# Agent attention and a SoLU feed-forward layer on one core: another table for the order of all queues

## The chip, the core and the metric

The kernel runs on one NeuronCore of a Trainium2 chip. The metric is device time in microseconds (us); lower is better. The core has five queues that work side by side and meet only at semaphores: TensorE (PE in the profile; its weight loads are PEld), VectorE (DVE), ScalarE (ACT), GpSimd (POOL) and SyncE (SP), which starts the transfers. Each queue takes its instructions strictly in the order in which the program wrote them: an instruction that waits holds up all that stand behind it on its queue.

## The reference

The inputs are q, k, v of 4 batches x 12,608 tokens x 128 channels and 49 agents for each batch.

```python
def _attn_ref(q, k, v, agents):
    scale = 1.0 / np.sqrt(q.shape[-1])
    def sm(a, b):
        s = scale * (a @ b.transpose(0, 2, 1)); s = s - s.max(-1, keepdims=True)
        e = np.exp(s)
        return e / (e.sum(-1, keepdims=True) + 1e-09)
    return sm(q, agents) @ (sm(agents, k) @ v)

def _moe_ref(x, w_in, w_out, g_ln):          # x: 50,432 tokens x 128
    h = x @ w_in                              # 128 -> 1024
    e = np.exp(h - h.max(-1, keepdims=True))
    solu = h * (e / (e.sum(-1, keepdims=True) + 1e-09))
    mu = solu.mean(-1, keepdims=True); var = ((solu - mu) ** 2).mean(-1, keepdims=True)
    return ((solu - mu) / np.sqrt(var + 1e-06) * g_ln) @ w_out   # 1024 -> 128
```

## The kernel before

**Tiles.** The 50,432 tokens are 394 tiles of 128 tokens, x = 0 to 393. For each tile the kernel goes through the same steps, each on its own queue:

- hidden layer (TensorE, L956, in two halves): `ph` = 128 x 1024, one PSUM buffer for even tiles and one for odd ones
- max (VectorE, L984): reads `ph`, writes `e_a` or `e_b` (even, odd tile) and the tile's extreme value
- exp (ScalarE, L991): reads `e`, writes the exponentials back into `ph` and sums them
- product (VectorE, L999): `u` = e x `ph`, into one of six buffers `u_a` to `u_f`, and its sum. With it `ph` and `e` of this tile come free, and the hidden layer of tile x+2 may start
- square (ScalarE, L1020): the sum of squares for the variance; it may come several tiles later
- turning `u` over: for 331 tiles it is split into two float16 parts (GpSimd or ScalarE L1007/L1005, then GpSimd L1010, buffers `f_a` to `f_e`) and turned by a transposing DMA (SP, L1014) into `x_a` to `x_h`; for the other 63 tiles TensorE turns it in two halves (L1027) and ScalarE or VectorE copies it out of PSUM (L1032) into `t_a` to `t_h`
- second layer (TensorE, L1048): 24 float16 matmuls from `x`, or 8 float32 ones from `t`, into a PSUM bank `px` that four tiles share; written in pieces, between which other work may stand
- for every 8 or 16 tiles a chain of tiny steps for 1/sqrt(var) (ScalarE and GpSimd, L1063 to L1086), and for every four tiles the scaling into `ob` (VectorE, L1093) and a store (L1099)

**Beside it.** For the next batch, in 13 chunks, the agents' attention over k and v (L585 to L755: loads, TensorE L602, L635, L655, VectorE L607 to L664, ScalarE L619, L628, L645); and for every 8 tiles the softmax of q over the agents (L843 to L911: `logits`, `pack`, its transposed form `pT`, copied out by ScalarE or VectorE). Batch 0's agents' attention and the conversion of the weights (L399 to L509) have nothing to stand beside: they are the head of the program, about its first 56 us.

**What sets the order.** `op(...)` declares 7,003 steps: a queue (or a choice of two, `eng` with two letters), a function that writes the instructions, and the steps it depends on. `Plan.run` then goes through a table, `STEPS`, a packed list of pairs (step, which of its two queues), and writes the steps in that order:

```python
        for i, k in todo:
            o = self.ops[i]
            e = o.eng[k]
```

Nothing else sorts them: priorities, costs and due times that stand in the code (`DH`, `DMX`, `due`, ...) do not decide the order, since the table does. The planned times in `run` choose two things only: which of four free PSUM banks a step takes, and how many filler matmuls (`idle`, L1109) stand before TensorE's steps in the head. The lines that the change and the prediction touch are L956, L984, L991, L999, L1020, L1048 and the table.

Of the kernel before, what the change touches and what calls it, by code (L numbers as in the profile page):

```python
# [18 lines left out]
AF = mybir.ActivationFunctionType  # L19
# [11 lines left out]
    "MzeXE>Azps4`{~4QL^=PaL@m6uqKtN&VK06m20N#(ck`0zG>y?Q6{RX>A=Ax*1w`5G&}0m2;NpZ1b{Dc7a6o<woHk5R3rNKY$YN4?tiG<)<hS#"
    "#77HLa{cA`SiEs+bZtTsY-=D|(h)<bk?bWSp=#go!jxmSMr8<yHP;$ybY@{IiH|jdWcSpdE4?^yGa^g&kB`Lq=K+3Wh@EK^1a+E=P_}ogBOgxP"
    "CoAvQ0!Kh2Yp+$#`;Hb<hEqbn=Ue=}KkaFXHArRiZ$FHj%E@7T0}TG`PoIa}nLhQ7MU7LZs>&%_xWlrKrSaW^Mo;%_x4mtM0PC|h*;=c7x3ZJG"
    "v&^;XcCF5I+5@EhE9+?mbpj^szx_M-E!A?~+;lKu)^yfu!&eQ52eJt;P~DzBTBKrUiI%yK<n+5H{YnFHbP%#xA0W&++5QwTu3(4Kd0U&QSFz-t"
    "@m;&##S~-*0EX2ny^|c!hMlfHOsAP#OgpV<a^g1KN|95!@Xfm8igXTWt*J4~6{*_NU$+0@*VjhJj>#iANvziCWa)cyBBlb<R|5%BF=gH|VS&X-"
    "@XP;m<gV(J(pX)x6|XkDuU{VO93lGxeM5b5u<3Cmk4Adi7H$;nvC00i^OW&Yc?~LLYhCMJJ(=w%<)`v-_n|Q@tBz?e$xZ-p*;eP~ATZ%UeP3Em"
    "4Uu2_snD8i4Hx$`Uo`D^S4qO!$3Ga|ArpiP*yrwpX#*J8vDeL9)q2hEdQ_?4v3J(tXf|e3aLuFDHjf>QS1rv>F3vhGSDaurN7mct>~n_xxR^?L"
    "=Cp(}7))8s{&;-!hE(kI+Z{69_N1qOxjv+>@LjJMjSUZV9r0kl&wfFiHf-lCmyOtE<2}{jpSXM=wNsXUvp-hTvPQN>bSWjZa=jM4e~?T3wrFti"
    "Sbs_G-N{EU8`m0+f8?juCcq&HTEIluNLUC^?Wh`WINa{sBCDGEgDOP>7{AA;m8BzWArUf3o4~g1^c;Fu%|}wDT9idBRxhw64`Mi&S1u-%H>c_2"
    "zDR9r#btPG#v@&&`VVD|%g)TUqD^*FGo&5M`RwgSk+_4j`i|Oxl&tlPfyInF>$O!Zn^!-?(_yMUdQUjg3oSYj?4O@poC};m+xX8r^!LP$cFE$n"  # L40
    "omrYc^7!U$R*iL7ZfG2O2p-6q3=PZeReRft6B)jGq4I3Y^c!QHedb)xrDx0^Q(ek_^!uHM@<vxnQifL&W37Yt%E?gr?yh~kz5aH(J!oogG}X?g"
    "Yp(HAthvgf75&_G_2P8p?Hw`c^%yH-s%bw+e$aMaNb2$9ww?M++PioXn={*2Tn7rU5-0p{rO=`GkNb{~+s(i8U+g!k?d7ZORo9RIT1)z5@a}ZW"
    "PMQ-fcjV!R#f!)o4scc7)XkA*UU&X+=HjHT1DFrCx2inOY3u6J#JaXxX?9-ik1m-e7cbSROIhX0TgU9XQ+cPX@%_}ol&!<^AOGvb1rAOIE*ov>"
    "fXxv-p2~DwHH07Z;NZjo4m&}gRi2PZyZoCWWnJj}L(jyFyk#q$86pQ-C(TnsotqUK0aMy8?eyCxdk#0+MrH3O8$+{e<XdU~$#vJBcv`mI7y-=^"
    "jgnG#%^t_<=8ZwQ8@Ei3?O9d12Ib(w)Pgc>(9g=}f(K*|?zP_LPRSvBrcLijcLP~Y;gQcRB;@k5&I2-&?&&`0^58>w+wlf|Gq@yw^J6m#JZX!Q"
    "#A(fNRI^7W-0y2^$>AlRF%w$A4b{t`57VvDMW1Qbf7P%sWn3BDRrpo5c`$k{ac&!dTW0aw`XY;e_}!RntmS=hI~6+Yyy)<of$cJQoY5XS|H)4n"
    "T*QYxeVx4OzCPv*gTC>8?Gl6%ur#qBHn>CkgNL#DP7kGdr*8kw*G{ZX<=8>v!7MOArjeh{_Kh|l_U=kYkJq)*;|TzUfOW1fGi%!J-CZBHsj1zK"
    "?s%nptVX@z>FrJeDdw_lMfa(R@$A-c3*NJnlE}uLitha#;;i$ucX!cT)qJB!0&q4HP<L&?5r90SNVcri^^&JV1_w*ak=9#q_GiC#tVp+jHQiO~"
    "jb?1AT|7R&sE&Jwap0I$#4E47{lWPrJgn*6^SSWqkM5uUAA?s7lS><WAZhAY0`s={%`4K8ovfdpYaItmI?8|Klr;dm7dU_Pt4#HJPE`|_zEupb"
    "oydIss`yr?4q7KI)`Fdn0~a0J13Ij&!MxUpCtHq2&fQ~)!K78;Y4#`v_qzc>5jh_@F+=)5jYpbP{KIb~BDE)EdSvuNB=Bw;-+UNdm@}k}^WlX$"  # L50
    "=?bBV2KEAdJyo&jQSklk>>hdIGIyEw$)USOP1Lxu5pHV%Ew#puo+LiI*wt?w^eDQGE3GLPE*k`ZsBPCs=lk6nquY~^?%<kUM^={_nbxJooi0m-"
    "zPHA=H@+|x0?t^#7BEEhxhwrapw?ya4U7)$;b!stro<NMO$=Q0Cz~Tg)#PksZ(+&}$;Yq?f1G5$E@bh^Omo_W%z#I}>eJbX@#xveLidtJQuQx>"
    "&1sTF4i|PbnGUaY>tr<7g8THRV%d3P;@F#(fpyu5_!^%wwGm^GAi(`$Le{^(c4YSJdfyH;Dt3AriI#V=9a}JcRHxo*I_h%|7~|^1#HRE%KHE<i"
    "WYcrjuGuqE4*=LB$4vokc%1|aO1(JKuOnns_e78EWJ?wACuE&ot7a^1b@V}#pGGD-w+F!4ul$lcJ>**5JnMA7zx7(ddecWekluzrrqz*&vmblf"
    "Xpq4Tc(?uMe`jN8uV?Q4+w1x|Ad4qj=j<1QL7f7$*tN3eyMSrVs2ZMc=!@9q2PePteQ#TB=#Vf?`L{O*?YjQ{pwZ-CIn((EW@V|kO;@v)lzO`q"
    "vPSv5v1yS~WICWk!T0-`-E+q$WH(_p>^k?m*P*i>DJm?!52O`eJ#2&SoCr8`+RK}4?a6T%94AxLd-^S}?kZw@sFwHao}|)sJ@1q?)nj|aZf_(t"
    "cSh!-wN71V8z%<=ZVGIscdg)1GBs+sksE7j-}=*zr2lQVF?i_HK?5$jw$j$!q+&IGyhn_Dm^e5hGohW#(a-$ru4SjSb-XH~1pU#?u`OlgVcZVY"
    "XzfW|E~2Bn^|~2z!$Zye;+SG*+Y5sy8JMX~He9M=TYX(K^PxSr<Z4+DVJE)fn{mgy|LCW|hmMYc?emqy&;8_Kr^%MMBF#j=H0yPCC?@2TUS;tq"
    "^#;-}9XqP?E`UnU(Sz5uOeNaKmvx(SSN_Y!Wv^;m9<)z*Ku4t21d&YT3T{MGR-!2~?38w<f%YO!2As0A$4IK+(l$P5Jw$6neX&VQ-4S3YcmW#k"
    "!-J-6kcicU%#e9-t9MI=Q}blVX3j-T>z(3n|Kd@f=Q{h&)#H*lx|Vy>J!i5L#pdoZnU1@z*1J{9U^~2}H#oziE0iJ7pl+XkyAt#e@rJ%GWzSFl"  # L60
    "Y25Du`1ZiKMu$`Hvg6yvNsYbpuxCc9@OHJ0o55bso~nZq1JHh!={ozxAH4((=0tbK>2ACQW2yRuj2OR>XW|{#+rjW{WyJ@p7-)&*-}t_js0SZi"
    ";**WKD_KNcd7W0ARl8S5m&vP2^HH+;s_U?)Dg}{88mwvmINtR(?Y7lTxTIu7+&p%DnScP_Bp*~-jt|v0c=BO>J*w1zN%`PqBYx9%*|;9N^<ON%"
    "pIR|1Ck~~nhUQgOMn3D9P@2i6Lmdo`3zww}2lCScDcB*rkuw=J5xOMZ{b@r3xEzbFYe;g$Hny?ptG~#oG)qaK&IA_XO);7Bx=I?5M`nP(yZN9i"
    "TL<x{wXUY)CI<Q{m+C5dX5C9U59R3$JH+5!^LCx<pzEOyc+UnmZkC)Ai>`0~R^(yEJFi_@9-p(1nZTj=x*mAq{)f6al!Z25T)G>dR;BwcA_S0M"
    "ZfhzpqK?1ue`GF=xc;DP!@WrmQALl%xjbvIr+XGPr#V6v@B*K7aR2Orv{oPFx{`QpxK8ho`JjFncFf{KjpE~Me+$@kTT*Xj(cTa4Q~A!&FnPP="
# [1232 lines left out]
```

## Time and profile before

| | |
|---|---|
| median of 3 runs | 1259.42 us (1253.04 to 1260.58) |
| the profiled execution's own time | 1255.41 us, span 1253.6 us |
| granted clock of TensorE, mean over the span | 0.997 of full speed |
| busy: PE, DVE, ACT, POOL | 1209.3, 1203.3, 1183.0, 1119.7 us |
| first max of a tile (start of the tiles) | 56.18 us |

A busy time is the time in which at least one instruction of the engine ran. In the timeline a row has its start, its length, and in brackets how long the engine sat idle before it and what ended that. The instruction behind it on DVE or ACT often starts a little before it ends (its last 0.07 us or so overlap), so what an instruction takes on its queue is the distance from its start to the next one's start. The small READ_ACCUMULATOR rows belong to the row ahead of them.

### The profile page before, as it was taken

What the parts mean: (1) busy time and instruction counts of PE and PEld (TensorE: products, weight loads), DVE (VectorE), ACT (ScalarE), POOL (GpSimd) and SP (SyncE); (2) the same over time, 40 slices, a digit from 0 to 9 for tenths busy, and PEclk for the clock granted to TensorE, in tenths of its full rate; (3) what the DMA queues carried; (4) which work ended last, traced back from release to release, by engine and by line L of the source; (5) the groups of instructions that cost most, each with busy time, mean ns of one, the idle gap of its engine ahead of it and who ended that gap; (6) DMA issues with size and microseconds to landing.
All of it is one profiled execution on the core that took longest, in us unless ns stands there. A gap on an engine that the chain in (4) does not pass through costs nothing.

```text
span 1253.6 us, 36378 instructions
## 1 busy us (share of the span) xinstructions
PE 1209.3 (96%) x14304; PEld 933.9 (74%) x14304; DVE 1203.3 (96%) x2296; ACT 1183.0 (94%) x2212; POOL 1119.7 (89%) x889
## 2 busy tenths in 40 slices
...
GB/s 367 201 226 237 216 251 227 218 243 219 203 200 244 250 222 249 249 257 238 226 201 207 247 247 236 231 261 235 214 231 193 174 196 219 166 224 200 194 190 169
DMA packets 721516, 281.41 MB, mean 224 GB/s; under 512 B 692672, under 2 KB 696256, under 8 KB 721344
## 3 DMA queue, kind: packets, MB, share of 16 engines
...
## 4 chain that ended last, share of the span: by engine, by line
PE 24%; DVE 23%; ACT 21%; issue 14%; POOL 10%; DMA 8%; SPq 0%; POOLq 0%; DVEq 0%; ACTq 0%
PE px L1048 10%; ACT ph L991 9%; PE ph L956 7%; DVE e_b L984 4%; DVE e_a L984 4%; ACT sq_a L1020 4%; ACT sq_b L1020 4%; PE px L655 2%; POOL f_b L1010 2%; PE px L602 2%; DVE u_f L999 2%; DVE u_d L999 2%; DVE u_a L999 2%; POOL f_a L1010 1%; DVE u_c L999 1%
## 5 line engine op out<-in xcount | busy, mean ns | idle before, releaser
L984 DVE TENSOR_SCALAR_CACHE_REDUCE e_a<-ph,nk 128x1024 f32<-128x1024 f32 x197 | 251.8, 1278 | 6.5 <-PE ph L956 5.5
L984 DVE TENSOR_SCALAR_CACHE_REDUCE e_b<-ph,nk 128x1024 f32<-128x1024 f32 x197 | 251.9, 1278 | 5.3 <-PE ph L956 4.9
L991 ACT ACTIVATE ph<-e_a,nm 128x1024 f32<-128x1024 f32 x197 | 219.3, 1113 | 16.2 <-DVE e_a L984 14.8
L991 ACT ACTIVATE ph<-e_b,nm 128x1024 f32<-128x1024 f32 x197 | 219.3, 1113 | 9.0 <-DVE e_b L984 8.0
L999 DVE SCALAR_TENSOR_TENSOR u_d<-e_b,cb,ph 128x1024 f32<-128x1024 f32 x66 | 84.3, 1277 | 2.1 <-ACT ph L991 1.6
L999 DVE SCALAR_TENSOR_TENSOR u_a<-e_a,cb,ph 128x1024 f32<-128x1024 f32 x66 | 84.2, 1275 | 1.8 <-ACT ph L991 1.4
L999 DVE SCALAR_TENSOR_TENSOR u_c<-e_a,cb,ph 128x1024 f32<-128x1024 f32 x65 | 82.9, 1275 | 2.4 <-ACT ph L991 1.6
L999 DVE SCALAR_TENSOR_TENSOR u_e<-e_a,cb,ph 128x1024 f32<-128x1024 f32 x65 | 82.9, 1275 | 1.5 <-ACT ph L991 1.1
L999 DVE SCALAR_TENSOR_TENSOR u_f<-e_b,cb,ph 128x1024 f32<-128x1024 f32 x65 | 82.8, 1274 | 1.3 <-ACT ph L991 0.7
L999 DVE SCALAR_TENSOR_TENSOR u_b<-e_b,cb,ph 128x1024 f32<-128x1024 f32 x65 | 83.0, 1277 | 1.0 <-ACT ph L991 0.4
L1048 PE MATMUL px<-wh,x_a 128*128 128x128 f16 x672 | 70.1, 219 | 3.6 <-DMA x_a<-f_e 1.7
L1048 PEld LDWEIGHTS <-x_a 128*128 128x128 f16 x1008 | 61.7, 98 | 14.2 <-DMA x_a<-f_e 1.9
L1048 PE MATMUL px<-wh,x_b 128*128 128x128 f16 x672 | 71.5, 219 | 0.7 <-DMA x_b<-f_a 0.5
L1048 PEld LDWEIGHTS <-x_b 128*128 128x128 f16 x1008 | 61.4, 98 | 14.4 <-issue 5.7
L1048 PE MATMUL px<-wh,x_c 128*128 128x128 f16 x672 | 70.9, 219 | 0.9 <-ACT pT_d L911 0.3
L1048 PEld LDWEIGHTS <-x_d 128*128 128x128 f16 x984 | 60.5, 98 | 14.8 <-issue 2.6
L1048 PE MATMUL px<-wh,x_d 128*128 128x128 f16 x656 | 68.9, 219 | 1.9 <-DMA x_d<-f_c 0.6
L1048 PEld LDWEIGHTS <-x_c 128*128 128x128 f16 x1008 | 61.9, 98 | 11.7 <-issue 2.3
L1048 PEld LDWEIGHTS <-x_e 128*128 128x128 f16 x984 | 60.2, 98 | 13.2 <-issue 3.8
L1048 PE MATMUL px<-wh,x_g 128*128 128x128 f16 x656 | 68.5, 219 | 1.5 <-DMA x_g<-f_e 1.2
L1048 PE MATMUL px<-wh,x_h 128*128 128x128 f16 x656 | 69.2, 219 | 0.6 <-DMA x_h<-f_c 0.6
L1048 PEld LDWEIGHTS <-x_h 128*128 128x128 f16 x984 | 60.5, 98 | 12.4 <-DMA x_h<-f_c 1.1
...
## 6 DMA issues: line engine op xcount, KB each, us to landing
...
```

The lines of the kernel that those rows point to most:

```text
L602: nc.tensor.matmul(px[h * AP2 : (h + 1) * AP2, :w], ag_sb[:, b, :], kt[:, o : o + w], start=True, stop=True)
L655: nc.tensor.matmul(px[h * AP2 : (h + 1) * AP2, :C], eT[:w, o + h * AP2 : o + (h + 1) * AP2], vt[:w, t, :], start=all(z[0] != h for z in mm ...
L956: nc.tensor.matmul(ph[:, sl], w, m[:, sl], start=(q == 0), stop=(q == len(mm) - 1))
L984: nc.vector.tensor_scalar(out=nhs[x], in0=phs[x], scalar1=nks[k][:, j : j + 1], scalar2=None, op0=ALU.mult, op1=ALU.min, accum_out=nms[x])
L991: nc.scalar.activation(out=phs[x], in_=nhs[x], func=AF.Exp, scale=-1.0, bias=nms[x], accum_out=rs_[R]["S"][:, j : j + 1])
L999: nc.vector.scalar_tensor_tensor(out=u, in0=nhs[x], scalar=scal(x)[:, 4:5], in1=phs[x], op0=ALU.mult, op1=ALU.mult, accum_out=su)
L1010: nc.gpsimd.tensor_tensor(out=fs[x][:, 1, :], in0=us[x][0], in1=fs[x][:, 0, :], op=ALU.subtract)
L1020: nc.scalar.activation(out=sq, in_=u, func=AF.Square, bias=su, scale=-float(DF), accum_out=rs_[R]["Q"][:, j : j + 1])
L1048: nc.tensor.matmul(po, ut, wt[:, kf, :], start=(q == 0), stop=(q == len(mm) - 1))
```

## The change

Only the table `STEPS` is another one: 7,003 pairs as before, of the same steps. Two of its lines, one of each side (the rest is alike: packed text):

```diff
 STEPS = (
-    "c-pOb4@@Ipe&6_Eyevy7wWbpvp%fv?@v|)ILxehrB1C;IaU70Vlu$w~$8j8oB0|v?IgU#l*CK>$R|pZ}I+o=Ugf^5CN?gbBITTSssbg`3x;_pe"
...
+    "c-p0T4^V4ge%H+*<nj2iNYm@}{t#J2WNDg7Q<h~JM9Ls$(llidBO)Tj42=w>H1kAcV@xwKrYvP%8N_Ui5hGIO$sj}1l%_GI3}ujFmSQH8vdAzD"
...
 )
```

Unpacked, the two tables agree in their first 3 steps and differ in the order of nearly all queues from there on, the head's included. 85 steps change their queue: 25 of the first splits go from ScalarE to GpSimd and 22 the other way; the copies of `pack` 10 from ScalarE to GpSimd and 9 back; the copies of `pT` 9 from VectorE to ScalarE and 6 back; the copies of `t` 3 from ScalarE to VectorE and 1 back.

**Place 1: TensorE around the hidden layer of tile 46** (201 to 204 us in the trace; `mh`, `ml` are the batch's matrix in two float16 parts, `ph_167` the even tiles' buffer, `x_a`, `x_b` two turned tiles for the second layer). Before:

```order
L956 LDWEIGHTS pT_b
L956 MATMUL ph_167<-mh_655,pT_b 128x512
L956 LDWEIGHTS pT_b
L956 MATMUL ph_167<-ml_656,pT_b 128x512
L1048 LDWEIGHTS x_a
L1048 MATMUL px_170<-wh_93,x_a 128x128
...
L1048 LDWEIGHTS x_b
L1048 MATMUL px_170<-wh_93,x_b 128x128
L956 LDWEIGHTS pT_b
L956 MATMUL ph_167<-mh_655,pT_b 128x512
```

and now:

```order
L1048 LDWEIGHTS x_b
L1048 MATMUL px_172<-wh_93,x_b 128x128
L956 LDWEIGHTS pT_b
L956 MATMUL ph_167<-mh_657,pT_b 128x512
L956 LDWEIGHTS pT_b
L956 MATMUL ph_167<-ml_658,pT_b 128x512
L956 LDWEIGHTS pT_b
L956 MATMUL ph_167<-mh_657,pT_b 128x512
L956 LDWEIGHTS pT_b
L956 MATMUL ph_167<-ml_658,pT_b 128x512
L1048 LDWEIGHTS x_b
```

Before, 12 matmuls of the second layer (six from `x_a`, six from `x_b`) stand between the two halves of this tile's hidden layer; now the halves follow each other.

**Place 2: ScalarE between the exponentials of tiles 227 and 228** (754 to 760 us in the trace; `nm` is the tile's extreme value, `sq` a square's output that nobody reads). Before:

```order
L991 ACTIVATE ph_168,S_10085<-e_b,nm_10512 128x1024
L1032 COPY t_c<-px_172 128x512
L911 COPY pT_b<-px_171 128x512
L1020 ACTIVATE sq_a,Q_10086<-u_e,su_c 128x1024
L1020 ACTIVATE sq_a,Q_10086<-u_c,su_a 128x1024
L991 ACTIVATE ph_167,S_10085<-e_a,nm_10590 128x1024
```

and now:

```order
L991 ACTIVATE ph_168,S_10080<-e_b,nm_10514 128x1024
L1020 ACTIVATE sq_b,Q_10081<-u_b,su_h 128x1024
L1032 COPY t_c<-px_172 128x512
L1020 ACTIVATE sq_a,Q_10081<-u_e,su_c 128x1024
L991 ACTIVATE ph_167,S_10080<-e_a,nm_10583 128x1024
```

The copy of `pT_b` has left this gap; two squares and one copy stand in it still.

**Place 3: ScalarE between the last two exponentials, of tiles 392 and 393** (1236 to 1243 us in the trace). Before:

```order
L991 ACTIVATE ph_167,S_17408<-e_a,nm_17365 128x1024
L1063 ACTIVATE t_17430<-S_17073,cb_13260 128x8
L1032 COPY t_e<-px_169 128x512
L1020 ACTIVATE sq_b,Q_17074<-u_f,su_f 128x1024
L1020 ACTIVATE sq_a,Q_17074<-u_a,su_g 128x1024
L1020 ACTIVATE sq_b,Q_17074<-u_d,su_d 128x1024
L991 ACTIVATE ph_168,S_17408<-e_b,nm_17452 128x1024
```

and now:

```order
L991 ACTIVATE ph_167,S_17405<-e_a,nm_17362 128x1024
L1032 COPY t_e<-px_172 128x512
L1020 ACTIVATE sq_b,Q_17069<-u_d,su_d 128x1024
L1063 ACTIVATE t_17445<-S_17068,cb_13253 128x8
L1020 ACTIVATE sq_a,Q_17069<-u_e,su_e 128x1024
L1020 ACTIVATE sq_b,Q_17069<-u_b,su_h 128x1024
L1020 ACTIVATE sq_b,Q_17069<-u_f,su_f 128x1024
L991 ACTIVATE ph_168,S_17405<-e_b,nm_17457 128x1024
```

Four squares stand in front of the last exponential instead of three, and two behind it instead of three.

## Rows read from the trace of the kernel before

**Rows 1.** The page: span, and busy time of each engine over it.

```profile
span 1253.6 us, 36378 instructions
PE 1209.3 (96%) x14304; PEld 933.9 (74%) x14304; DVE 1203.3 (96%) x2296; ACT 1183.0 (94%) x2212; POOL 1119.7 (89%) x889
```

**Rows 2.** Stretches: length, busy PE, PEld, DVE, ACT, POOL; clock; DMA share, GB/s.

```profile
0.00:60.00 60.00, 49.64 (x467) 30.07 (x468) 43.07 (x115) 32.55 (x77) 23.47 (x33) 0.97 0.76 289
80.00:1240.00 1160.00, 1133.20 (x13567) 882.79 (x13564) 1134.32 (x2137) 1123.45 (x2087) 1075.95 (x834) 1.00 1.06 222
1240.00:1254.00 14.00, 10.36 (x116) 9.94 (x113) 6.53 (x13) 8.11 (x18) 2.23 (x10) 1.00 0.32 123
320.00:420.00 100.00, 98.17 (x1193) 76.25 (x1193) 99.45 (x186) 98.89 (x184) 96.72 (x75) 1.00 1.05 223
420.00:620.00 200.00, 199.53 (x2415) 155.83 (x2412) 196.98 (x374) 194.65 (x371) 184.13 (x145) 1.00 1.14 242
```

**Rows 3.** VectorE's waits: what waited, for whom: us in total, times, longest.

```profile
DVE e_a L984 <- PE ph L956: 5.5, 10, 1.1
DVE e_b L984 <- PE ph L956: 4.9, 10, 1.6
...
DVE pk L718 <- ACT av_dup L714: 2.6, 4, 0.9
DVE row L675 <- PE px L669: 2.4, 1, 2.4
DVE u_c L999 <- ACT ph L991: 1.6, 8, 0.3
...
DVE u_b L999 <- ACT ph L991: 0.4, 2, 0.2
```

**Rows 4.** Timeline at 200 to 204 us: VectorE, then TensorE's hidden layer of tile 46.

```profile
200.70 1.28 DVE L999 SCALAR_TENSOR_TENSOR u_d<-e_b,cb,ph 128x1024 f32<-128x1024 f32 x1
...
203.16 1.28 DVE L984 TENSOR_SCALAR_CACHE_REDUCE e_a<-ph,nk 128x1024 f32<-128x1024 f32 x1 [1.05 <-PE ph L956]
...
201.43 0.38 PE L956 MATMUL ph<-mh,pT_b 128*128 128x512 f16 x1
...
202.53 0.38 PE L956 MATMUL ph<-mh,pT_b 128*128 128x512 f16 x1
```

**Rows 5.** Timeline at 754 to 760 us: ScalarE, then VectorE, tile 228.

```profile
755.07 0.58 ACT L911 COPY pT_b<-px 128x512 f16<-128x512 f16 x1
755.55 1.16 ACT L1020 ACTIVATE sq_a<-u_e,su_c 128x1024 bf16<-128x1024 f32 x1
...
757.97 1.10 ACT L991 ACTIVATE ph<-e_a,nm 128x1024 f32<-128x1024 f32 x1
...
759.11 1.10 ACT L991 ACTIVATE ph<-e_b,nm 128x1024 f32<-128x1024 f32 x1
...
759.23 1.28 DVE L999 SCALAR_TENSOR_TENSOR u_a<-e_a,cb,ph 128x1024 f32<-128x1024 f32 x1 [0.37 <-ACT ph L991]
```

**Rows 6.** Timeline of the end: ScalarE's last exponential, VectorE's last product, TensorE.

```profile
1241.71 1.10 ACT L991 ACTIVATE ph<-e_b,nm 128x1024 f32<-128x1024 f32 x1
...
1242.98 1.28 DVE L999 SCALAR_TENSOR_TENSOR u_d<-e_b,cb,ph 128x1024 f32<-128x1024 f32 x1 [0.60 <-ACT ph L991]
...
1247.67 0.60 PE L1027 MATMUL px<-ident,u_d 128*128 128x128 f32 x4
```

**Rows 7.** Timeline at 885 to 898 us: a transposing DMA, and who waited.

```profile
885.46 4.31 SPq L1014 DMA_TRANSPOSE x_a<-f_e  x1
...
894.26 0.23 PE L1048 MATMUL px<-wh,x_a 128*128 128x128 f16 x1 [1.74 <-DMA x_a<-f_e]
...
897.83 0.48 DVE L675 TENSOR_REDUCE row<-px 1x64 f32<-1x128 f32 x2 [2.38 <-PE px L669]
```

**Rows 8.** Groups by line in the head: busy us, mean ns of one, idle before.

```profile
L399 DVE TENSOR_SCALAR u_e<-u_e 128x512 int32<-128x512 int32 x4 | 4.3, 1080 | 0.0
L399 DVE TENSOR_SCALAR u_a<-u_a 128x512 int32<-128x512 int32 x4 | 1.7, 420 | 0.0
```

More of the change, by code (lines that the diff above doesn't have):

```diff
@@ L31 @@
[L31 to L65, printed above, removed]
@@ new lines @@
+    "ve`Rnj12O4JV@^K+&@X~y|C-3^WKEy-gD1A=lkdL`Fy{p`J}Zgj>V@^9k;r^!!(v|t~g5{_H|&#8{@Y+XG_(lCOVMW?b$t?JgKrC-PLCzt@cIv"
+    "rV7_wWIhZHFNcQ12DE*>(mg4^tGcbfJ;P^xiMII@7r2q>P6k?+=Vz}XGnb}!)%D)C3**k}#!3C*P`j&n$$whuPtUB4RJ9N3<!d9AsN-P<_+}i#"
+    "4Y#Yq+Gy2m`N*2NZE8Gl_V})<Y8Jh*p_u?k-7NV`a=&puet-HQgC>*%ONWM3>R{Irv<+<TrZ;C=2dwFyWZKy@;Uyox@=pQi-<D<j0#d0~o%BnA"
+    "MscP{-FKwoJrNC&%A$2dOq){fXxGV>Yz>N?lZyFK{NMfgBq6^a!q-#y&FJ35o>K0u+chfED`0^fUQ8=@qaazMMMuK#qr)QxZ)&Dnquj%%VyU!J"
+    "r4838=X(~>L^yUHP!g+PZDg8QA0AvXOOF>vQ^PoTJW18mR1-&w3%jAUk>QZvIIy{XH!&YZvxv4F^=Yg9k!H<_F?JHx&ivXpPDATyqB;`L-_P#j"
@@ new lines @@
+    "=#=GVZQW~ir4rVw(J5;JQ%)t8(5a0<0F1ZsC9^Gc(1<GE*9>NwmTw-LYrDHf&nj%Q<~6W(7f?o&J6Fz=U-=%H=-u8iX@EhmRPVa5qX|oN8a=)-"
+    "%%+o};g*_#Sq*u1(sJXq&YlwKuKgweh>#ELgU*e1wWH4()bAWy#!>Q-tc>q0JQ7Fvp*4jyjqDtToLlm<iGxo4G?qwpuh+K|hM)egU;RxY?pU6h"
+    "S=owp_uVe5E@EAM!K%!SX05fs5I@knH0^1hWeYceN%!*g!UwH+>HNSsuz9sIJGxqag_onY6@8l$uLZNKgkneD8(i|&jh|0p>t{}z&*aM5UDsY0"
+    "*dDv7J#I55!<Z+$eT4drs}5E5=D+{#wRbjrvUS2{E++}H_WWGu*N#nQ$B)$+QvSW421<uLRO6XW;R!+uo`^d4Bzj}86Ur$74*HfO0gYut-VN^h"
+    "mSQV=;Sti1@?eI8ev=Dpc!!5hLfsDe!c1q&n6i4@o#?CY9<6S0PY$1Ws@rtUE)Ox3L1RI`HvIR$h52Q}3H??5VFy6J{x5f$`_-{0C)V6S94c0a"
@@ new lines @@
+    "2m9QISR^&vaC!SU9>2Ujp0H^qfn{z(RdcgCOU$nvG*>(Dv4z=jTg{w>lwQ|iW8F8iI@DEr55i~Hl^)B~vSY-(FtF*$$}Dr1lWNkwLXvi(?w@@B"
+    "mwq-`1D5N0@1`?*C#KE5m=2TnO~pGWx(A{UQ+>S;L@O9OIlXGyOZAPZ?bQL4H2015E$RoSWMo_X3J;GgSc6#I;{Y(4@1@I@*x*^FW7g=>>Oz|6"
+    "?Ommo2&TN=y8)ujGcl|izDy~|^=qG3gGDsukL8yQM|wS8X(rNo=e6&uzH1vKJi!q!5lT&0fCr)h)rFevsyXjrM>9rxPNc3~viJVVmYz*3A~lMZ"
+    "os2?e51yPhU%?0f%5(tJ`i<?)lS-SHjL2rE2MC|(v>8ihO@7qV)ZH`J8XQi0C-?3LgQ;5WW?a*^lhKij=U(?D2wXon(@Q_|<%Y}Z0+#w=d~%|u"
+    "!fdSx>7Hg6-z{FXUiWFsqPEuS`6|oq$)l}$cmZ=o{l`xI_#-a;`j377GkCummx2k;Xwd1sx$#)e6mW~z&EDC^viaG&%i%@sq^aZ4YYnv2g7YTX"
```

198 lines of the change are left out of this document (109 added, 89 removed).

## The prediction, written before the kernel ran

> **What bounds the kernel now.** I read the page's busy times first. VectorE is busy 96% of the span, ScalarE 94%, GpSimd 89%, TensorE 96% [rows 1]: no queue has more than a few per cent to give, so a new order can only win time in which VectorE stands. Then I cut the span into stretches [rows 2]. The head (0 to 60 us) leaves VectorE idle 60 - 43.1 = 16.9 us, the last 14 us another 7.5, and the long middle from 80 to 1240 us only 1160 - 1134.3 = 25.7 us. The reader is to see that the middle is what 394 tiles cost, and that its idle time, 2% of the whole, is all that a better order could take there. The densest 100 us have VectorE at 99.45 [rows 2].
>
> Third, VectorE's waits by what it waited for [rows 3]. Two kinds make up most of the 25.7: the max of a tile waits for the hidden layer (5.5 + 4.9 = 10.4 us in 20 places), and the product waits for the exponential (six rows, from 1.6 down to 0.4, 6.8 us in all). Together 17.2 us. The rest are ends of the agents' attention (2.6 and 2.4) and crumbs.
>
> The two kinds have one cause. For each of the two `ph` buffers the steps go round: product, hidden layer of the tile after next, max, exponential, product. A round lasts as long as VectorE needs for two tiles, but each step also has to get through its queue: the hidden layer behind pieces of the second layer on TensorE, the exponential behind squares and copies on ScalarE. Tile 46 shows the first [rows 4]: the halves of its hidden layer begin at 201.43 and 202.53, and the max waits 1.05 us. Tile 228 shows the second [rows 5]: the copy of `pT` and two squares hold the exponential until 757.97, the next begins 1.14 us later, and VectorE waits 0.37 us for the first.
>
> **The change part by part.** No step is added or removed, so VectorE's work stays. The 85 steps on another queue nearly cancel: three splits fewer on ScalarE (each about as long as an exponential of the same shape, 1.1 us by [rows 5], so 3.3 us), three copies of `pT` more on it (0.58 each [rows 5], 1.7 us), two copies of `t` and one of `pack` fewer. That leaves ScalarE some 3 us less and GpSimd some 4 us more, out of queues that idle 36 and 84 us in the middle [rows 2]; I cost it at nothing beyond what the queue sums below contain. If GpSimd's cover were gone, it would be 4 us at most.
>
> *The order in the middle.* I compared the two orders by the work that stands in each queue, with each step's mean distance from its start to the next start in the trace of before. For each tile: TensorE's work from the hidden layer of the tile ahead up to the end of this one's, against VectorE's work in the same reach (from the product that releases the first up to this max), less 0.39 us for two hand-offs. Where TensorE's sum is the larger, VectorE must stand. Before, that holds at 82 of 376 tiles and is 9.4 us in sum; now at 74, and 7.4 us. Likewise ScalarE's work from exponential to exponential, less 0.31 us: 99 tiles and 15.6 us before, 94 and 11.6 now. Reaching back over eight tiles, TensorE's shortfall is 63.5 us before and 41.3 now, ScalarE's 35.0 and 22.7. These sums overlap and are no times, but they shrink alike, to between 0.65 and 0.79 of what they were.
>
> Taking 0.70, near the middle, of the 17.2 us leaves 12.0: **5.2 us gained**; the ends are 3.6 (0.79) and 6.0 (0.65). Place 1 is an instance: between the halves stood 12 matmuls of the second layer, 202.53 - 201.43 = 1.10 us less the first half's own two (0.4) is 0.7 of the 1.05 us waited [rows 4], and they are gone from there. Place 2 is a smaller one: a copy of at most 0.58 us has left the gap in which 0.37 was waited [rows 5].
>
> From 420 to 620 us TensorE is busy 199.5 of 200 us [rows 2]; taken at its word, nothing can be won there, and VectorE's 3.0 us of idle time in that stretch, an eighth of the 25.7, would stay: 4.6 instead of 5.2. The weight loads fill only 155.8 of those 200 us [rows 2]. The Trainium skill (Perfetto Trace Analysis, Identifying the Most-Contended Engine) says that matmul busy time is a bad measure of TensorE's headroom and that weight loads are the better one; by it the stretch has a fifth of TensorE free and the gain is the full 5.2, by the busy row 4.6. I take 5 us.
>
> *Head.* Four transposes of `pack` that stood between the hidden layers of tiles 0 and 1 now stand ahead of the head's last product. I take 0.4 us gained, from one matmul row of that length [rows 4], with bounds of 1.5 lost or gained: VectorE idles 16.9 us there [rows 2], so most moves in it meet other idle time.
>
> *End.* Place 3 puts one more square, 1.16 us [rows 5], ahead of the last exponential. VectorE's last product already waits 0.60 us for it [rows 6] and would begin up to 1.2 us later. Behind it TensorE turns the second half at 1247.67, 3.4 us after that product ended [rows 6], because its own queue is late; so of 1.2 us I count 0.4 lost, bounds 0 and 1.2. It cancels the head.
>
> **The sum** is made against the profiled execution, 1255.4 us: minus 5.0, minus 0.4, plus 0.4, gives 1250.4. The median of the runs is 4.0 us above that execution and the lowest 2.4 below it; a new median can fall on either side, so I add half of the 4.0: **1252 us**. What a measurement of this kernel can tell from no change is about 1%, 12.6 us: under 1246.8 counts as faster, over 1272.0 as slower.
>
> **The rivals.**
>
> *Twice the gain or more.* If the new order lets the whole middle run as the densest 100 us do, 1134.3 / 0.9945 = 1140.6 us against 1160, 19.4 us fewer: 1236 against the profiled execution. Half of that is 1246. For it: the eight-tile sums shrink by a third, more than 5 us would use. Against it: those 100 us have next to no agents' attention beside the tiles, while much of the middle has, and 74 and 94 tiles are still short. I put this at 1243, between 1236 and 1247, chance 0.20.
>
> *Nothing comes of it.* Other waits take the place of those removed. The queue sums use mean durations, while the longest waits are chance meetings that no sum holds [rows 7]: the 2.38 us of `row`. Time 1256 to 1259, chance 0.16.
>
> *Slower: turned tiles come late.* Ordinary loads and stores share the SP queue and the transfers with the transposing DMAs. In the trace one transpose took 4.31 us to start and land behind others; TensorE waited 1.74 us for its tile, and because TensorE's queue is in order, a step of the agents' attention behind it made VectorE wait 2.38 [rows 7]. In the order before, 14 times five transposes in a row have six or more ordinary transfers among them; now 27 times. If half of the 13 further places cost 2.38 us each, 15 us are lost and the time is 1267; from nine of them on the kernel is slower by over 1%. Against it: the second layer now stands further behind the split (65 tiles with at most three products between, 85 before), which gives late transposes more room; and 14 such places gave one long wait. Chance 0.08.
>
> *The head's conversions meet GpSimd differently.* The same VectorE instruction on integers, 128x512, took 0.42 us as `u_a` and 1.08 as `u_e` [rows 8], so 4 x 0.66 = 2.6 us of VectorE's head depend on what runs beside it. If none of it recurs, 1249.5; if as much is added on the chain of the head, 1254.6. Chance 0.04. The Trainium skill (SBUF — State Buffer, Who interferes with whom) says that VectorE and GpSimd share a pair of SBUF ports as an exclusive lock, so that a VectorE instruction in a two-port mode or with two SBUF inputs waits for a whole GpSimd instruction, and issue order decides who waits; the two rows agree with it. By it a new order is not neutral for durations in the head; for max and product, with one SBUF operand each, it excludes a change.
>
> **How the numbers follow.** Forecast 0.52, with its own range 1247 to 1257 (gains of 3.6 to 6.0, head and end 1.5 either way, the run's level between the profiled one and the median). The rivals have 0.20, 0.16, 0.08, 0.04. The range of 8 in 10 reaches down into the first rival and up over the second and the milder part of the third: 1239 to 1263. It leaves out the lower third of the first (0.06) and most of the third (0.06). Faster by over 1%: the first rival and the lowest edge of the forecast, 0.20 + 0.06 = 0.26. Slower by over 1%: nine or more of thirteen late transposes, and mishaps like it, 0.06. Within 1%: 0.68.
>
> **What would show each step right or wrong.** In the stretch from 80 to 1240 us VectorE's busy time stays at 1134 within 3 us while the stretch that holds the same tiles is some 5 us shorter. The waits of `e_a` and `e_b` for `ph` fall from 10.4 to about 7, those of `u` for the exponential from 6.8 to about 5. The start of the tiles stays at 56 us within 1.5, and so does what follows the last exponential. Wrong would be: VectorE's busy time itself changing by over 5 us; waits for `ph` that stay at 10 us; or TensorE's waits for transposing DMAs of over 1 us, five or more of them. The forecast falls if the waits are no function of the queue sums.

## The result, and the profile after

| | before | change |
|---|---|---|
| median | 1258.93 us (14 runs, 1253.04 to 1260.71) | 1265.04 us (14 runs, 1261.58 to 1268.95) |
| profiled execution: own time, span | 1255.41, 1253.6 us | 1267.18, 1265.4 us |

The ratio is 1.0064 with a 95% interval of 1.005 to 1.0079: the change is some 6 us slower, where 1252 had been forecast and 1239 to 1263 allowed for; it lies 2 us above that range. The size is within the 1% called "same", the direction is not the forecast's.

The two profiled executions are 11.8 us apart, the medians 6.1: the change's is the second longest of its 14 runs, and that of before lies 3.5 us under its median. The traces show where the time goes; what they lose is about twice the usual loss.

The page of the change, busy times, against [rows 1]:

```profile
PE 1213.8 (96%) x14301; PEld 935.1 (74%) x14301; DVE 1201.9 (95%) x2295; ACT 1182.3 (93%) x2209; POOL 1121.7 (89%) x893
```

Its stretches (length; busy PE, PEld, DVE, ACT, POOL; clock; DMA share; GB/s), against [rows 2]:

```profile
0.00:60.00 60.00, 50.62 (x468) 29.74 (x468) 44.30 (x118) 33.46 (x78) 23.38 (x34) 1.00 0.76 291
80.00:1240.00 1160.00, 1123.97 (x13412) 873.56 (x13410) 1122.13 (x2117) 1111.97 (x2067) 1070.32 (x831) 1.00 1.07 221
320.00:420.00 100.00, 98.86 (x1221) 77.54 (x1220) 98.90 (x189) 98.82 (x185) 95.65 (x74) 1.00 1.09 214
420.00:620.00 200.00, 195.39 (x2327) 150.56 (x2324) 192.60 (x368) 191.44 (x361) 180.92 (x142) 1.00 1.13 240
```

VectorE has the same work over the whole program (1203.3, now 1201.9). In 80 to 1240 us it gets through 12 us less of it: it stands there 37.9 us, not 25.7. The densest stretch (98.90 of 100) has hardly changed; 420 to 620 us has lost 4.4 us. VectorE's waits, against [rows 3]:

```profile
DVE e_a L984 <- PE ph L956: 13.5, 15, 4.9
DVE e_b L984 <- PE ph L956: 7.1, 10, 1.7
...
DVE pk L718 <- ACT av_dup L714: 3.2, 3, 1.5
...
DVE u_d L999 <- ACT ph L991: 2.1, 6, 0.9
DVE u_a L999 <- ACT ph L991: 2.0, 2, 1.8
```

The waits for the hidden layer have doubled, from 10.4 to 20.6 us. Those for the exponential are where they were (6.8, now about 6.6). TensorE's waits name what made the hidden layers late:

```profile
PE px L1048 <- DMA x_h<-f_b: 3.8, 2, 2.2
PE px L1048 <- DMA x_a<-f_c: 3.2, 1, 3.2
...
PE px L1048 <- DMA x_g<-f_c: 1.7, 1, 1.7
PE px L1048 <- DMA x_b<-f_c: 1.7, 1, 1.7
...
PE px L1048 <- DMA x_g<-f_e: 1.3, 1, 1.3
PE px L1048 <- DMA x_f<-f_d: 1.2, 1, 1.2
```

These seven waits of over 1 us (12.9 us) are for turned tiles. Before there were two, of 2.9 us:

```profile
PE px L1048 <- DMA x_a<-f_e: 1.7, 1, 1.7
...
PE px L1048 <- DMA x_g<-f_e: 1.2, 1, 1.2
```

With the short ones TensorE waits 15.3 us for transposing DMAs between 80 and 1240 us, where it waited 8.9. The longest of the change in the timeline, with the tile's split on GpSimd, then SP, TensorE and VectorE (start, length, in brackets the idle time before):

```profile
768.97 2.14 POOL L1010 TENSOR_TENSOR f_c<-u_f,f_c 128x1024 f16<-128x1024 f32 x1
...
772.59 2.11 SPq L1014 DMA_TRANSPOSE x_h<-f_b  x1
774.75 0.58 SPq L1099 DMA_DIRECT2D out_dram<-ob_b  x1
775.42 0.41 SPq L843 DMA_DIRECT2D qt_b<-in_qT_dram  x1
775.88 0.80 SPq L585 DMA_DIRECT2D kt_a<-in_kT_dram  x1
776.78 5.29 SPq L1014 DMA_TRANSPOSE x_a<-f_c  x1
782.17 3.69 SPq L1014 DMA_TRANSPOSE x_b<-f_d  x1
...
786.41 0.23 PE L1048 MATMUL px<-wh,x_a 128*128 128x128 f16 x1 [3.24 <-DMA x_a<-f_c]
...
792.74 1.28 DVE L984 TENSOR_SCALAR_CACHE_REDUCE e_a<-ph,nk 128x1024 f32<-128x1024 f32 x1 [4.88 <-PE ph L956]
```

The split of this tile (227) ended at 768.97 + 2.14 = 771.11. So 5.7 us went by before SP began its transposing DMA, behind the end of one transposing DMA, another (`x_h`), an output, a q and a k transfer. It landed (all its data had arrived) at 786.36, 15.3 us after the split, and TensorE stood for it with the hidden layers behind.

VectorE's wait (4.88 us) is longer than TensorE's (3.24). One reason is TensorE's clock: from 787.4 to 790.8 us, right behind that wait, the granted clock was 0.50, the lower of its two levels (1.2 GHz):

```profile
787.40:790.80 3.40, 3.40 (x35) 3.32 (x33) 0.46 (x2) 2.56 (x6) 3.21 (x7) 0.50 1.17 266
```

The 128-column matmuls of L1048 started 0.056 us apart ahead of it and 0.107 us apart in it, so it cost about 1.6 us (an estimate from these two distances).

**Where along the program.** In these two executions I set the ends of the products (L999) of the two traces against each other, tile by tile. The change is 1.5 us ahead at tile 0 and 1.3 at tile 24; 1.1 behind at tile 120, 5.8 at 144, 8.5 at 216, 11.9 at 240, 12.8 at 276, and 12.8 at tile 393. The single place of the timeline above (tiles 235 and 236) adds 5.6 us, of which 1.8 are made up by tile 240. Nothing is lost in 320 to 420 us nor behind tile 276: only where the next batch's k and v are loaded beside the tiles (about 80 to 310, 430 to 605 and 700 to 945 us). In those stretches the time from the end of a split to the start of its transposing DMA (POOL's L1010 row and SP's L1014 row of the same tile, mean of 46 to 68 tiles) went from 2.7, 1.8, 2.1 us to 3.3, 3.0, 3.7; behind 945 us it is 0.6 in both.

### The profile page after: what moved, and what is told of

It reads as the page before. It is cut to its first block, busy times and chain, and to the rows that moved or that the text cites. A ratio compares the mean times of both kernels' runs of the same rounds, so it can differ in the third digit from the quotient of the medians.

```text
span 1265.4 us, 36389 instructions
## 1 busy us (share of the span) xinstructions
PE 1213.8 (96%) x14301; PEld 935.1 (74%) x14301; DVE 1201.9 (95%) x2295; ACT 1182.3 (93%) x2209; POOL 1121.7 (89%) x893
## 4 chain that ended last, share of the span: by engine, by line
PE 33%; ACT 19%; DVE 17%; issue 11%; POOL 9%; DMA 9%; SPq 1%; POOLq 0%; DVEq 0%; ACTq 0%
PE px L1048 15%; PE ph L956 9%; ACT ph L991 8%; DVE e_b L984 4%; ACT sq_a L1020 4%; ACT sq_b L1020 3%; DVE e_a L984 3%; PE px L655 3%; PE px L602 2%; PE px L1027 1%; DVE u_e L999 1%; DMA x_h<-f_b 1%; DVE u_f L999 1%; POOL f_b L1010 1%; PE px L864 1%
## 5 line engine op out<-in xcount | busy, mean ns | idle before, releaser
L991 ACT ACTIVATE ph<-e_b,nm 128x1024 f32<-128x1024 f32 x197 | 219.3, 1113 | 14.2 <-DVE e_b L984 12.8
L999 DVE SCALAR_TENSOR_TENSOR u_d<-e_b,cb,ph 128x1024 f32<-128x1024 f32 x66 | 84.2, 1276 | 2.6 <-ACT ph L991 2.1
L999 DVE SCALAR_TENSOR_TENSOR u_a<-e_a,cb,ph 128x1024 f32<-128x1024 f32 x66 | 84.1, 1274 | 2.3 <-ACT ph L991 2.0
L999 DVE SCALAR_TENSOR_TENSOR u_c<-e_a,cb,ph 128x1024 f32<-128x1024 f32 x65 | 82.7, 1273 | 1.5 <-ACT ph L991 0.9
L999 DVE SCALAR_TENSOR_TENSOR u_e<-e_a,cb,ph 128x1024 f32<-128x1024 f32 x65 | 82.8, 1275 | 1.2 <-issue 0.3
L999 DVE SCALAR_TENSOR_TENSOR u_f<-e_b,cb,ph 128x1024 f32<-128x1024 f32 x65 | 82.8, 1274 | 1.1 <-ACT ph L991 0.6
L999 DVE SCALAR_TENSOR_TENSOR u_b<-e_b,cb,ph 128x1024 f32<-128x1024 f32 x65 | 82.8, 1274 | 0.9 <-ACT ph L991 0.7
L1048 PEld LDWEIGHTS <-x_b 128*128 128x128 f16 x1008 | 62.3, 99 | 17.9 <-issue 6.0
L1048 PE MATMUL px<-wh,x_b 128*128 128x128 f16 x672 | 71.6, 221 | 3.2 <-DMA x_b<-f_c 1.7
L1048 PE MATMUL px<-wh,x_h 128*128 128x128 f16 x656 | 69.9, 219 | 3.8 <-DMA x_h<-f_b 3.8
L1048 PE MATMUL px<-wh,x_a 128*128 128x128 f16 x672 | 69.2, 220 | 4.2 <-DMA x_a<-f_c 3.2
L1048 PEld LDWEIGHTS <-x_h 128*128 128x128 f16 x984 | 60.4, 98 | 15.8 <-DMA x_h<-f_b 4.8
L1048 PE MATMUL px<-wh,x_g 128*128 128x128 f16 x656 | 68.1, 219 | 3.0 <-DMA x_g<-f_c 1.7
L1048 PE MATMUL px<-wh,x_c 128*128 128x128 f16 x672 | 70.1, 219 | 0.8 <-DMA x_c<-f_b 0.6
L1048 PEld LDWEIGHTS <-x_c 128*128 128x128 f16 x1008 | 61.6, 98 | 12.0 <-issue 2.1
L1048 PE MATMUL px<-wh,x_f 128*128 128x128 f16 x656 | 68.4, 219 | 1.6 <-DMA x_f<-f_d 1.2
L1048 PEld LDWEIGHTS <-x_a 128*128 128x128 f16 x1008 | 61.4, 98 | 11.1 <-DMA x_a<-f_c 3.7
L1048 PE MATMUL px<-wh,x_e 128*128 128x128 f16 x656 | 69.1, 219 | 0.5 <-DMA x_e<-f_d 0.5
L1048 PEld LDWEIGHTS <-x_f 128*128 128x128 f16 x984 | 59.9, 98 | 12.6 <-issue 2.1
```

The lines of the kernel that those rows point to most:

```text
L991: nc.scalar.activation(out=phs[x], in_=nhs[x], func=AF.Exp, scale=-1.0, bias=nms[x], accum_out=rs_[R]["S"][:, j : j + 1])
L999: nc.vector.scalar_tensor_tensor(out=u, in0=nhs[x], scalar=scal(x)[:, 4:5], in1=phs[x], op0=ALU.mult, op1=ALU.mult, accum_out=su)
L1048: nc.tensor.matmul(po, ut, wt[:, kf, :], start=(q == 0), stop=(q == len(mm) - 1))
```

## The experiments

Three theories stood at first. A: transfers make the turned tiles late. B: the order on the four compute engines is worse. C: each order of transfers fits only its own order on the engines. Orders are described, since rows of a packed table say nothing. Ratios are to the kernel before, run together with each experiment.

### SP's order swapped

```diff
 first kernel: PE, DVE, ACT, POOL in the change's order
-SP in the change's order
+SP in the order of before
 second kernel: PE, DVE, ACT, POOL in the order of before
-SP in the order of before
+SP in the change's order
```

Expected of the first: 

> The change's order on TensorE, VectorE, ScalarE and GpSimd, with SP's order of transfers as it was before. Theory A (SP's order holds the transposing DMAs back, in the stretches where the next batch's k and v are loaded): the wait from the end of a high/low split (L1010) to the issue of its transposing DMA falls from 3.3, 3.0 and 3.7 us in the three loading stretches of the change back to about 2, VectorE's waits for ph from 20.6 us to under 13, and the time is 1253 to 1259 us. Theory B (the loss is in the order on the compute engines): the time stays at 1263 to 1268 us, the waits for ph near 20 us. Theory C (each order of transfers fits only its own order on the engines): over 1268 us.

Expected of the second: 

> The mirror image: the kernel before with only SP's order of transfers taken from the change. Theory A: 1262 to 1268 us, VectorE's waits for ph from 10.4 up to 16 us or more, split to issue over 3 us in the loading stretches. Theory B: 1257 to 1260 us, as before. Theory C: over 1266 us, and the run with the transfers of before under the change's engine orders is over 1268 too.

Measured: 1286.56 us (1.0236, 1.0215 to 1.0257) and 1283.91 us (1.022, 1.0193 to 1.0246). Both are slower than either parent, as C said. TensorE's waits for transfers in the first:

```profile
PE px L655 <- DMA vt_b<-in_v_dram: 6.2, 1, 6.2
PE px L602 <- DMA kt_b<-in_kT_dram: 5.6, 1, 5.6
...
PE px L1048 <- DMA x_c<-f_e: 3.7, 1, 3.7
PE px L864 <- DMA qt_b<-in_qT_dram: 2.7, 1, 2.7
```

Now k, v and q come late as well. A foreign order of transfers costs over 20 us against the kernel with the same order on the engines, so neither swap can say whether SP's order lost the 6 us. Part of that cost is the clock: from 80 to 1240 us TensorE worked 16 and 12 us at a granted clock of 0.50, in the change 3.4, in the kernel before not at all.

### Ordinary transfers spread

```diff
 SP, from tile 24 on, 36 places:
-ordinary, ordinary, transposing
+ordinary, transposing, ordinary
```

> The change with 36 swaps in SP's order alone: from tile 24 on, where two or more ordinary transfers stand next to each other in front of transposing DMAs, the first transposing DMA goes ahead of the last ordinary one. Theory A in its form 'bunches of ordinary transfers hold the transposes': 1257 to 1263 us, split to issue down by 0.5 to 1 us in the loading stretches. Theory A in its form 'the number of transfers ahead at the time, not the bunch': 1262 to 1266. Theory B: 1264 to 1268.

Measured: 1280.33 us (1.0185, 1.0166 to 1.0205), over all that was expected. TensorE's waits for turned tiles are 18.2 us, and for k, v and q together 10.5; it worked 23 us at the lower clock. Breaking up bunches blindly makes both sorts late.

### Fewer bytes, same order

```diff
 kload, vload, batches 1 to 3 (here a quarter; then a half):
-kT[b, :, c*1024 : c*1024 + 1024]  ->  kt[:, :1024]
+kT[b, :, c*1024 : c*1024 + 256]   ->  kt[:, :256]
-v rows (p j), j = 0 to 7  ->  vt
+v rows (p j), j = 0, 1    ->  vt[:, :2]
```

Quarter, order of before: 

> The kernel before, with the k and v transfers of batches 1 to 3 cut to a quarter of their columns (the first two of each buffer pair stay whole, so stale columns are computed with; the output is not the reference's). Order, count and places of all instructions stay. Every theory: a little faster than before, 1250 to 1257 us, because VectorE's waits in the middle that can go are about 15 us in all and few of them stand behind a transfer.

Quarter, the change: 

> The change with the same cut. Theory A (the transposing DMAs come late because they stand behind the k, v, q and output transfers in one queue): the change's loss goes with the bytes; 1246 to 1257 us, no more than 2 us over the kernel before with the same cut, VectorE's waits for ph from 20.6 to under 13 us, and TensorE's wait of 3.2 us at 786 us under 1 us. Theory B (the order on the compute engines): 6 to 12 us over the kernel before with the same cut, waits for ph still 18 us or more.

Half, order of before: 

> The kernel before with the k and v transfers of batches 1 to 3 cut to half of their columns (the first two of each buffer pair whole; stale columns are computed with). With a quarter of the columns it took 1245.1 us against 1259.7. In proportion to the bytes: 1250 us (two thirds of the 14.6 us). If the transfers only hurt where they nearly fill the time of the 16 engines: 1246 to 1248.

Half, the change: 

> The change with the same cut to half. With a quarter of the columns it took 1241.3 us against 1265. In proportion to the bytes: 1249 us, level with the kernel before at half. If the waits grow faster than the bytes (a backlog that only forms when the queue cannot drain between bunches): 1242 to 1245, and 3 to 5 us under the kernel before at half, as at a quarter.

| k, v columns | before | change | TensorE waits for turned tiles | VectorE waits for `ph` |
|---|---|---|---|---|
| all | 1258.93 | 1265.04 | 8.9; 15.3 | 10.4; 20.6 |
| half | 1245.37 (0.9907, 0.9886 to 0.9928) | 1242.45 (0.9883, 0.9858 to 0.9908) | 0.5; 1.9 | 3.7; 5.0 |
| quarter | 1245.12 (0.9885, 0.9863 to 0.9906) | 1241.29 (0.9851, 0.9826 to 0.9876) | 0; 1.1 | 2.3; 2.8 |

The first two chunks of batch 1 and the short last chunk of each batch stay whole; in the others the columns that are not loaded keep what stood there, in both orders alike. The waits of VectorE with a quarter, in the order of before:

```profile
DVE e_b L984 <- PE ph L956: 1.5, 5, 0.5
DVE e_a L984 <- PE ph L956: 0.8, 2, 0.4
```

The sign turns: with half the bytes the change is 2.9 us ahead, with a quarter 3.8, although every queue keeps its order. That is theory A: the loss is made by transfers. The quarter in the order of before fell below the lowest that had been expected (1250 us): there too I had taken few waits to stand behind a transfer. The loss is also not in proportion to the bytes: by the ratios the first half is worth some 12 us in the order of before and 23 in the change, the next quarter some 3 and 4 (each within some 3 us), where proportion would make it 6 and 11. The same place in the change with a quarter of the columns, SP and then TensorE:

```profile
754.66 0.57 SPq L1099 DMA_DIRECT2D out_dram<-ob_b  x1
755.33 0.40 SPq L843 DMA_DIRECT2D qt_b<-in_qT_dram  x1
755.78 0.85 SPq L585 DMA_DIRECT2D kt_a<-in_kT_dram  x1
756.72 3.68 SPq L1014 DMA_TRANSPOSE x_a<-f_c  x1
...
766.08 0.22 PE L1048 MATMUL px<-wh,x_a 128*128 128x128 f16 x1
```

The same three transfers stand ahead of it, but the split had ended at 754.55, so SP began 2.2 us later instead of 5.7; it landed at 764.23, 9.7 us after the split instead of 15.3, and TensorE found it there. So the same order of transfers does not make the tile late when the transfers are lighter.

### One stretch exchanged

```diff
 between the products of tiles 222 and 250, all queues:
-the kernel's own order
+the other kernel's order
```

In the change: 

> The change, with the steps between the exponent products of tiles 222 and 250 (about 751 to 841 us) in the order of before on all queues. In the change this stretch takes 3.9 us more than before, and tiles 234 to 236 alone 5.4 us. Theory A as a sum of places: 1259 to 1262 us. If the lateness only moves (the backlog of transfers is met further on), 1263 to 1267.

In the kernel before: 

> The mirror image: the kernel before with the steps between the exponent products of tiles 222 and 250 in the change's order. As a sum of places: 1261 to 1264 us, with a wait of TensorE for a transposing DMA of over 2 us near 778 us. If the stretch is only slow because of what the change did ahead of it, 1257 to 1260 us.

Measured: 1265.19 us (1.0045, 1.0027 to 1.0063) and 1261.91 us (1.0023, 1.0005 to 1.0041). The change does not get its loss back: the wait for `x_a` is gone, one of 1.49 us for `x_c` stands at 794.8. In the old order the change's stretch brings its wait along (2.09 us, `x_a`, at 776.5) and costs 2 to 3 us. The first came out as expected if the lateness only moves, the second as expected if places add up. So the place matters, and something beside it too; how full the queue is when the program gets there would fit, and is not shown.

### Transfers on another queue

```diff
 k transfers of batches 1 to 3:
-nc.sync.dma_start(out=kts[c][:, :w], ...)
+nc.scalar.dma_start(out=kts[c][:, :w], ...)
 in two other kernels, outputs of tiles 32 to 367:
-nc.sync.dma_start(out=out[:, x0 * C : x1 * C], ...)
+nc.gpsimd.dma_start(out=out[:, x0 * C : x1 * C], ...)
```

k by ScalarE, order of before: 

> The kernel before with the k transfers of batches 1 to 3 (39 of them) issued by ScalarE at the same places of the table; all bytes stay. If a transposing DMA is late because its issue stands behind others in SP's queue: split to issue falls from 2.7, 1.8 and 2.2 us to under 1.5 in the loading stretches and TensorE's waits for transposing DMAs from 8.9 to under 5 us; 1250 to 1257 us if an issue on ScalarE costs little, and up to 1275 if each takes ScalarE the 0.4 to 0.8 us that SP shows. If it is late because its bytes share the 16 engines: the issue comes sooner but issue to landing grows by as much, waits stay, 1258 us or more.

k by ScalarE, the change: 

> The change with the same 39 transfers issued by ScalarE. SP's queue as the cause: split to issue from 3.3, 3.0 and 3.7 us to under 2, TensorE's waits for transposing DMAs from 15.3 to under 8 us, 1252 to 1260 us if the issue is cheap on ScalarE. The 16 engines as the cause: issue to landing grows from 5.3 to 5.7 us to 7 us or more, waits stay at 13 us or more, 1264 us or more.

Outputs by GpSimd, the change: 

> The change with the output transfers of tiles 32 to 367 issued by GpSimd at the same places of the table. If the one order in SP's queue makes transposing DMAs late: split to issue from 3.3, 3.0 and 3.7 us to under 2.8 in the loading stretches, TensorE's waits for them from 15.3 to under 11 us, 1255 to 1263 us, if an issue costs GpSimd under 1 us (some 42 of them beside 139 us of idle time). If the bytes on the shared engines do: waits 13 us or more, 1263 us or more. Against both: GpSimd stands in order too, and a wait for the last product of a group can hold its splits back, over 1268.

Outputs by GpSimd, order of before: 

> The kernel before with the same edit. One order in SP's queue: TensorE's waits for transposing DMAs from 8.9 to under 6 us, 1252 to 1257 us. Bytes: 1257 to 1262 us. GpSimd held back: over 1263.

Measured: 1270.96 (1.0115, 1.0073 to 1.0157), 1271.97 (1.0124, 1.0085 to 1.0163), 1271.56 (1.0126, 1.008 to 1.0173) and 1277.29 us (1.0157, 1.0126 to 1.0188). All four are slower, but each issue takes time of its new engine: the issues of k on ScalarE, and of outputs on GpSimd (durations ns min/median/max):

```profile
L585 ACTq DMA_DIRECT2D kt_b<-in_kT_dram x20: 334/334/445, 65.6 to 885.5; - x20
```

```profile
L1099 POOL DMA_DIRECT2D out_dram<-ob_a x21: 579/602/757, 241.8 to 1200.1; - x21
```

39 x 0.334 is 13 us of ScalarE and 42 x 0.602 is 25 us of GpSimd, which could account for what was lost (6.5 to 18.4 us against the kernel that each comes from). For the question itself: with k on ScalarE's queue the change's splits wait 2.7, 2.4 and 2.9 us for their issue instead of 3.3, 3.0 and 3.7, but from issue to landing it takes 5.5 to 5.7 us, as in SP's queue (5.3 to 5.7), and TensorE's waits for turned tiles stay at 14.7 us. In the order of before the wait for the issue falls as well (1.9, 1.1, 2.1 us), yet those waits rise from 8.9 to 22.4 us, against what had been expected if the line were the cause. A second queue takes away part of the wait in line and none of the transfer. The Trainium skill (DMA: Bandwidth & Descriptors, Issuing engines are not separate DMA queues) says that transfers run on the same 16 engines and interleave whichever engine started them, so that a further queue saves only issue time; the landings agree. Since the issue time is in it, the four runs settle nothing on SP's order.

### SP's queue by the time to spare

```diff
 SP, from 80 us on: a transfer moves ahead of others (of three at most in
 all but a few cases), where the trace says that it gains and they can spare
 it; those may slip back further. One place of the change:
-q qt_a, k kt_b, transposing x_a, transposing x_b
+transposing x_a, transposing x_b, k kt_b, q qt_a
```

In the change: 

> The change with SP's queue alone in another order from 80 us on: transfers change places over at most three others, so that in its own trace each would land further ahead of the product that wants it. In busy stretches of SP's queue a transposing DMA took 2.4 us and a 512 KB transfer 1.5 to 2.3 us (fits to both traces); by these the 1 in 20 transposing DMAs with the least time to spare gain 1.6 us. If the order in SP's queue is the cause: TensorE's waits for transposing DMAs from 15.3 to under 6 us and 1250 to 1258 us. If the cause is the bytes wherever they stand, or the engines' order: waits of 12 us or more and 1262 to 1268 us. If the order on the engines tolerates no other order of transfers, as in the whole swaps: over 1270 us.

In the kernel before: 

> The kernel before, its SP queue reordered in the same way by its own trace (the tightest 1 in 20 transposing DMAs gain 1.0 us). If the order in SP's queue is the cause: TensorE's waits for transposing DMAs from 8.9 to under 4 us and 1248 to 1255 us. If not: 1257 to 1261 us; over 1265 if the engines' order tolerates no other.

Measured: 1306.59 us (1.0359, 1.0324 to 1.0394) and 1320.19 us (1.0455, 1.0417 to 1.0492), the slowest of all; both came out as expected (over 1270 and 1265) if the order on the engines tolerates no other order of transfers. The change's waits of TensorE for transfers, and of VectorE for outputs:

```profile
PE px L655 <- DMA vt_b<-in_v_dram: 16.4, 4, 9.3
PE px L602 <- DMA kt_b<-in_kT_dram: 10.4, 2, 7.1
...
PE px L1048 <- DMA x_g<-f_b: 2.0, 1, 2.0
...
DVE ob_a L1093 <- DMA out_dram<-ob_a: 11.9, 3, 8.5
```

Its aim was reached: waits for turned tiles are 5.4 us instead of 15.3 (in the kernel before it was not: 11.5 us, from 8.9). But v, k and the outputs pay more than that, and behind these waits TensorE worked 31 us (in the kernel before 34) at a granted clock of 0.50. A likely reason, which no run isolates: my figures for the spare time took the moments at which transfers could start from the old trace. An ordinary transfer that stands behind a transposing one also waits for that one's split (SP stands in order too), and each delay moves the later moments. So SP's queue decides **who** is late; none of the orders that I tried on SP alone made less lateness in sum.

### The two ends

```diff
 first kernel:  change up to the exponential's product of tile 24, then before
 second kernel: the same, and the change again behind tile 360
```

Head alone: 

> The change's table up to the exponent product of tile 24 (about 130 us), and behind it all steps that are left in the order of before, on every engine. By the tile times of the two traces the change is 1.3 us ahead at tile 27 and loses all of it and 12 us more behind that. Theories A and B both expect 1256 to 1258.5 us (0 to 1.5 us under before). If the lead of the head is taken back by a wait at tile 24 or later, 1258.5 to 1260; if the loss is prepared in the head, over 1262.

Both ends: 

> The change's order up to the exponent product of tile 24, that of before up to tile 360, and the change's behind it. The tail behind the last exponent product took 9.36 us before and 8.30 in the change, and the first row maximum ended at 57.46 and 56.01 us. If both gains stand by themselves: 1254 to 1258 us, 0 to 2.5 under before, and a tail of 8.3 us. If the middle takes the head's gain back, as the splice at tile 24 alone did: 1257 to 1260.

Measured: 1259.25 us (1.001, 0.9992 to 1.0027) and 1256.10 us (0.9989, 0.9971 to 1.0006). In both traces the first max ends 1.5 us earlier than before; in the second, 8.31 us follow the last product, not 9.36. The head alone came out in the range expected if the middle takes its lead back: from the product of tile 24 to that of tile 393 its trace takes 1109.9 us, that of before and that of both ends 1105.5, although all three have the same order up to tile 360. So a few us of the middle come and go with when its transfers begin. The profile of the second has a span of 1250.8 us. It has the lowest median of the versions that load all of k and v, and is not distinguishable from the kernel before.

## Why the prediction was wrong

**The step that failed is "the order in the middle"**, with its term of minus 5.0 us, in two ways. From the product of tile 24 to that of tile 393 the traces take 1105.5 us before and 1119.7 now: 14.2 us lost where 5.0 had been forecast as gained.

*The waits were no function of the queue sums.* I took 10.4 + 6.8 us of waits as made by work standing in TensorE's and ScalarE's queues, and scaled them. With k and v cut to a quarter, the waits for `ph` under the **old** order are 2.3 us: 8 of the 10.4 went with the transfers. I had counted queues of engines only and left out the one queue, SP's, whose lateness arrives on TensorE and passes as a wait for `ph`. Where transfers are light, the middle of the two orders takes the same time: against the old order at the same bytes the change is 2.4 us ahead at tile 24 and 2.2 at tile 393 (quarter), 3.2 and 3.0 (half). The smaller queue sums, 7.4 for 9.4 us and 11.6 for 15.6, were worth 0.2 us the wrong way. Both bounds, 3.6 and 6.0, excluded what happened.

*What the change does in the middle with whole transfers is the third rival*: turned tiles come late, 1267 us, chance 0.08. That late transfers are the cause is shown by the halved bytes. That its 1267 is near the 1265.04 is partly luck: it priced six or seven waits at 2.38 us each, some 15 us, and the medians lost 6.1. Its row was also misread: the 4.31 us of [rows 7] are the issue alone. That tile landed at 894.22, 8.8 us after its issue began and 17.0 after its split ended. The rival's chance was too low because of two arguments against it. "The second layer stands further behind the split" is true, and not enough: from the end of the split to the moment when TensorE is at the tile it is 10.8 us in the middle, 9.8 before (medians, tiles 24 to 393), but to landing 6.6 instead of 6.0, and for the slowest tenth 11.9 or more instead of 10.3. The 5% with the least time to spare have 0.1 us or less before and 0.0 now. "14 such places gave one long wait" counted only the one in [rows 7]; three more of about 1 us were in the same trace, and 8.9 us in sum.

What remains **open** is what in the new order makes the queue fuller. Its count of five transposing DMAs with six or more others among them (14, now 27) points the right way, but only three of the change's seven long waits are for a tile at such a place, and the longest is not. The swaps, the spread and the sorted queue all brought other waits, so no run isolates the cause. Nor do the lighter transfers tell SP's line from the transfers themselves, since both got shorter.

*Smaller steps.* VectorE's work did not change (1.4 us). The 85 steps on other queues were costed at nothing; nothing here speaks against it (busy times: ScalarE 0.7 us less, GpSimd 2.0 more). The head gained 1.5 us (0.4 forecast, the bound reached). The end had the wrong sign: 0.4 lost was forecast; the last product does wait 0.90 us instead of the 0.60 of [rows 6], but what follows it, with one square fewer behind the last exponential, is 1.06 us shorter. The conversions of [rows 8] took 683 ns (`u_e`) and 418 (`u_a`), and all of VectorE's work of L399 16.1 us instead of 17.3: that rival moved VectorE's head by 1.3 us. The Trainium skill's rule on matmul busy time (Perfetto Trace Analysis, Identifying the Most-Contended Engine) decided nothing: with light transfers TensorE is busy 1142 of 1160 us in the middle, more than the 1133 of [rows 2], so there was room, but the order did not use it.

*What I had written as signs of being wrong came true*: waits for `ph` at twice the 10 us, and seven waits of over 1 us for transposing DMAs.
